# Pairs of batches woven together in a chunk-attention and token-mixing kernel on one core

## The chip, the cores and the metric

The kernel runs on one core of one Trainium2 chip. The metric is the device time of one execution in microseconds, as the median of the runs. A core has a matrix engine (PE, with its weight loads PEld), a vector engine (DVE), a scalar engine (ACT), GpSimd (POOL, which here issues every load) and SyncE (SP, which issues every store). Matrix products are written to PSUM, eight banks of 2 KB per partition, and have to be moved out by DVE or ACT.

## What is computed

Eight batches, eight heads, 576 tokens, 64 columns per head. Attention works within chunks of 64 tokens; its output, 512 columns per token, goes through a mixing block whose four weight matrices all batches share.

```python
scores = q_c @ k_c.T / 8                    # per chunk of 64 tokens and head
attn = exp(scores - max) / sum
x = (attn @ v_c)  ->  [b, 576, 512]
theta = x @ w_theta
zr, zi = x * cos(theta), x * sin(theta)
y = w_tok_r @ zr + w_tok_i @ zi             # over the 576 tokens of a batch
u = x + y
out = u + max(u @ w_ch, 0)
```

## The kernel before

All products are in fp16 with fp32 sums. The 576 tokens of a batch are cut into four tiles of 128 and one of 64 (`NSB` = 5). The kernel has three stages, one after the other.

*Weights* (lines 62 to 92). POOL loads all four matrices; the two token matrices are turned by 50 PE transposes (L78), and DVE copies them out.

*Attention*, all batches (from line 96). For each batch 15 loads (L107) bring q, k and v; 40 PE transposes (L120) turn q and k, and DVE copies them out (L127, L130). Per head, nine 64x64 score products go to PSUM (L142), ACT takes the exponential (L147 for four tiles, L153 for the last half tile), and nine products with a column of ones give the sums (L161). The products with v (L180) are scaled by the reciprocals (L167, L170) into `x16` (L185), which is kept for all batches.

*Mixing*, all batches (from line 190). Per batch: 20 transposes of x (L202), copied by ACT (L207); 20 products for theta (L219); cosine and sine on ACT (L226, L230); zr and zi on DVE (L234, L237); 50 products of 512 columns for y (L251), with the weights' token tiles as the stationary side, so that the half tile of 64 tokens is met both as a row and as a column; the sum u (L259); 20 transposes of u (L269), copied by ACT (L274); 20 products with `w_ch` (L282); relu and sum on DVE (L290); store on SP (L294). PSUM tiles are one bank each and there are eight of them.

No order is written out by hand: a scheduler takes the instructions in the order of the program text as priorities, simulates when each can run and how tiles come free, and fixes each engine's order. An engine then works through its own list strictly.

Of the kernel before, what the change touches and what calls it, by code (L numbers as in the profile page):

```python
# [9 lines left out]
FP32 = mybir.dt.float32  # L10
FP16 = mybir.dt.float16
AF = mybir.ActivationFunctionType
ALU = mybir.AluOpType


@with_exitstack
def kernel(
# [11 lines left out]
    nc = tc.nc  # L29
# [3 lines left out]
    NC = S // CH  # L33
    P = 128
    NSB = (S + P - 1) // P
    SB_SZ = [min(P, S - P * i) for i in range(NSB)]
    NDB = DM // P
    NE = H // 2
    scale = 1.0 / math.sqrt(D)
    pi_half = math.pi / 2.0  # L40
# [3 lines left out]
    xpool = ctx.enter_context(tc.tile_pool(name="xpool", bufs=1))  # L44
    psum = ctx.enter_context(tc.tile_pool(name="psum", bufs=8, space=bass.MemoryType.PSUM))
# [3 lines left out]
    ones16 = const.tile([P, 1], FP16, name="ones16")  # L49
    nc.vector.memset(ones16, 1.0)  # L50
    pihalf = const.tile([P, 1], FP32, name="pihalf")
    nc.vector.memset(pihalf, pi_half)
    zerob = const.tile([P, 1], FP32, name="zerob")
    nc.vector.memset(zerob, 0.0)
# [3 lines left out]
    wtokT_r = glob.tile([P, NSB, S], FP16, name="wtokTr")  # L58
    wtokT_i = glob.tile([P, NSB, S], FP16, name="wtokTi")

    with tc.tile_pool(name="wstage", bufs=1) as wstage:
        for ap, f16 in ((moe_w_theta, wtheta16), (moe_w_ch, wch16)):
            nc.gpsimd.dma_start(f16, ap.rearrange("(a p) e -> p a e", p=P))
        for ap, res in ((moe_w_tok_r, wtokT_r), (moe_w_tok_i, wtokT_i)):
            f16 = wstage.tile([P, NSB, S], FP16, name="wtok_nat16", tag="wtok_nat16")
            nc.gpsimd.dma_start(
                f16[:, 0 : NSB - 1, :],
                ap[0 : (NSB - 1) * P, :].rearrange("(a p) s -> p a s", p=P),
            )
            nc.gpsimd.dma_start(  # L70
                f16[0 : SB_SZ[NSB - 1], NSB - 1, :], ap[(NSB - 1) * P : S, :]
            )
            for sblk in range(NSB):
                ns = SB_SZ[sblk]
                pst = psum.tile([P, NSB, P], FP16, name="ps_wtokT", tag="ps")
                for tb in range(NSB):
                    nt = SB_SZ[tb]
                    nc.tensor.transpose(  # L78
                        pst[0:ns, tb, 0:nt],
                        f16[0:nt, tb, sblk * P : sblk * P + ns],  # L80
                        id16[0:nt, 0:nt],
                    )
                nc.vector.tensor_copy(
                    out=res[0:ns, sblk, 0 : (NSB - 1) * P].rearrange(
                        "p (a s) -> p a s", a=NSB - 1
                    ),
                    in_=pst[0:ns, 0 : NSB - 1, :],
                )
                nc.vector.tensor_copy(
                    out=res[0:ns, sblk, (NSB - 1) * P : S],  # L90
                    in_=pst[0:ns, NSB - 1, 0 : SB_SZ[NSB - 1]],
                )

    x16 = [xpool.tile([P, NSB, DM], FP16, name=f"x16_{b}") for b in range(B)]

    with (
        tc.tile_pool(name="att", bufs=2) as att,
        tc.tile_pool(name="qkv", bufs=2) as qkv,
    ):
        for b in range(B):  # L100
            qk16 = qkv.tile([P, NSB, 2, H, D], FP16, name="qk16")
            v16 = qkv.tile([P, NSB, H, D], FP16, name="v16")
            for sb in range(NSB):
                ns = SB_SZ[sb]
                for ti, t_ap in enumerate((q, k, v)):
                    dst = qk16[0:ns, sb, ti] if ti < 2 else v16[0:ns, sb]
                    nc.gpsimd.dma_start(  # L107
                        dst,
                        t_ap[b, :, sb * P : sb * P + ns, :].rearrange(
                            "h s d -> s h d"  # L110
                        ),
                    )
            qT = att.tile([P, NE, S], FP16, name="qT")
            kT = att.tile([P, NE, S], FP16, name="kT")
            for sb in range(NSB):
                ns = SB_SZ[sb]
                pqk = psum.tile([P, 2, NE, P], FP16, name="ps_qkT", tag="ps")
                for which in range(2):
                    for e in range(NE):
                        nc.tensor.transpose(  # L120
                            pqk[:, which, e, 0:ns],
                            qk16[0:ns, sb, which, 2 * e : 2 * e + 2, :].rearrange(
                                "s h d -> s (h d)"
                            ),
                            id16[0:ns, 0:ns],
                        )
                nc.vector.tensor_copy(  # L127
                    out=qT[:, :, sb * P : sb * P + ns], in_=pqk[:, 0, :, 0:ns]
                )
                nc.vector.tensor_copy(  # L130
                    out=kT[:, :, sb * P : sb * P + ns], in_=pqk[:, 1, :, 0:ns]
                )

            eT = att.tile([P, H, NSB, CH], FP16, name="eT")
            ps_rs = psum.tile([P, NSB, H], FP32, name="ps_rs", tag="ps")
            for h in range(H):
                e, par = h // 2, h % 2
                pst = psum.tile([P, NSB, CH], FP32, name="ps_sT", tag="ps")
                for c in range(NC):
                    cb, cp = c // 2, c % 2  # L140
                    sl = slice(c * CH, c * CH + CH)
                    nc.tensor.matmul(  # L142
                        pst[cp * CH : cp * CH + CH, cb, :],
                        kT[par * D : par * D + D, e, sl],
                        qT[par * D : par * D + D, e, sl],
                    )
                nc.scalar.activation(  # L147
                    out=eT[:, h, 0 : NSB - 1, :],
                    in_=pst[:, 0 : NSB - 1, :],
                    func=AF.Exp,  # L150
                    scale=scale,
                )
                nc.scalar.activation(  # L153
                    out=eT[0:CH, h, NSB - 1, :],
                    in_=pst[0:CH, NSB - 1, :],
                    func=AF.Exp,
                    scale=scale,
                )
                for c in range(NC):
                    cb, cp = c // 2, c % 2  # L160
                    nc.tensor.matmul(  # L161
                        ps_rs[cp * CH : cp * CH + CH, cb, h : h + 1],
                        eT[cp * CH : cp * CH + CH, h, cb, :],
                        ones16[cp * CH : cp * CH + CH, :],
                    )
            recip = att.tile([P, NSB, H], FP32, name="recip")
            nc.vector.reciprocal(  # L167
                out=recip[:, 0 : NSB - 1, :], in_=ps_rs[:, 0 : NSB - 1, :]
            )
            nc.vector.reciprocal(  # L170
                out=recip[0:CH, NSB - 1, :], in_=ps_rs[0:CH, NSB - 1, :]
            )

            for sb in range(NSB):
                ns = SB_SZ[sb]
                npar = ns // CH
                psx = psum.tile([P, H, D], FP32, name="ps_xout", tag="ps")
                for h in range(H):
                    for cp in range(npar):
                        nc.tensor.matmul(  # L180
                            psx[cp * CH : cp * CH + CH, h, :],
                            eT[cp * CH : cp * CH + CH, h, sb, :],
                            v16[cp * CH : cp * CH + CH, sb, h, :],
                        )
                nc.vector.tensor_tensor(  # L185
                    out=x16[b][0:ns, sb, :].rearrange("s (h d) -> s h d", h=H),
                    in0=psx[0:ns],
                    in1=recip[0:ns, sb, :].unsqueeze(-1).broadcast_to((ns, H, D)),
                    op=ALU.mult,
                )  # L190

    with (
        tc.tile_pool(name="moe", bufs=2) as moe,
        tc.tile_pool(name="moew", bufs=2) as moew,
    ):
        for b in range(B):
            xT = moe.tile([P, NDB, S], FP16, name="xT")
            for sb in range(NSB):
                ns = SB_SZ[sb]
                pxt = psum.tile([P, NDB, P], FP16, name="ps_xT", tag="ps")  # L200
                for db in range(NDB):
                    nc.tensor.transpose(  # L202
                        pxt[:, db, 0:ns],
# [121 lines left out]
```

## Time and profile before

| | |
|---|---|
| median of two runs | 332.54 us (331.72 and 333.35) |
| span of the profiled execution | 329.0 us |
| time outside the span (median less span) | 3.5 us |
| PE busy | 285.2 us, 87% of the span |
| DVE, ACT, POOL busy | 146.2, 115.7, 105.4 us |
| mean granted clock of PE | 0.887 of full |

The span runs from the first to the last instruction of one profiled execution. The profiled execution's own device time is not given apart; beside its span of 329.0 us stands the median of the runs, 3.5 us more, and that difference is taken as what lies around a span. Busy shares are means over stages with different limits, so the rows below are read stage by stage.

### The profile page before, as it was taken

The page shows a single profiled execution, that of the slowest core. Times are in us where ns is not written, and L with a number is a line of the kernel's source. Part 1 is how long each engine was busy: PE and PEld are TensorE (multiplying, and loading weights), DVE is VectorE, ACT ScalarE, POOL GpSimd, SP SyncE. Part 2 cuts the span into 40 slices and gives each one's busy share as a digit, 9 for nine tenths or more (in the row PEclk, how much of TensorE's full clock was granted, in tenths as well). Part 3 has the DMA queues.
Part 4 walks back from the last instruction along what each step waited for, and adds up shares of the span by engine and source line. Part 5 has one row for each costly group of instructions (what it writes and reads, how often), then busy time and mean ns, then how long its engine had stood idle before and what let it go on. Part 6 is the DMA issues. An engine that isn't in the chain of part 4 may idle for free.

```text
span 329.0 us, 7260 instructions
## 1 busy us (share of the span) xinstructions
PE 285.2 (87%) x3138; PEld 159.2 (48%) x3138; DVE 146.2 (44%) x319; ACT 115.7 (35%) x290; POOL 105.4 (32%) x132
## 2 busy tenths in 40 slices
PE   0328977879869889999999999999999999999992
PEld 0216866768858777334344344344344344344340
DVE  0216437357347354544534625525535534533532
ACT  0001440431421424805615515425426326227220
POOL 8189999999999900000000000000000000000000
PEclk9999577575676576999999999999999999999998
DMA  6999999999999980003003004004004003003004
GB/s 107 175 134 152 146 138 138 149 142 140 151 138 144 147 44 3 2 0 130 16 0 131 16 0 140 5 0 145 0 0 146 0 0 131 14 1 129 15 1 144
DMA packets 120064, 26.44 MB, mean 80 GB/s; under 512 B 113248, under 2 KB 115424, under 8 KB 120032
## 3 DMA queue, kind: packets, MB, share of 16 engines
q0 software_dynamic: 114784, 16.54, 79.4%
q1 hardware_dynamic: 5248, 9.44, 8.4%
q8 instruction: 24, 0.39, 0.5%
q14 instruction: 8, 0.07, 0.1%
HBM read 33.06 MB, written 9.44 MB: 129 GB/s over the span
## 4 chain that ended last, share of the span: by engine, by line
PE 62%; POOL 14%; DMA 12%; DVE 7%; issue 2%; ACT 1%; DVEq 0%; POOLq 0%; ACTq 0%
PE ps_y L251 30%; POOL qk L107 9%; PE ps_theta L219 8%; PE ps_uw L282 8%; DMA out_dram<-o 5%; POOL v L107 5%; DMA wtok_nat<-in_moe_w_tok_r_dram 3%; PE ps_uT L269 3%; PE ps_sT L142 3%; PE ps_xT L202 2%; PE ps_rs L161 2%; PE ps_wtokT L78 2%; DVE o L290 2%; DMA wtok_nat<-in_moe_w_tok_i_dram 2%; DMA qk<-in_q_dram 2%
## 5 line engine op out<-in xcount | busy, mean ns | idle before, releaser
L251 PE MATMUL ps_y<-zr,wtokTr 128*128 128x512 f16 (+3 forms) x200 | 53.9, 382 | 0.7 <-DVE zr L234 0.6
L251 PE MATMUL ps_y<-zi,wtokTi 128*128 128x512 f16 (+3 forms) x200 | 54.5, 384 | 0.0
L259 DVE TENSOR_TENSOR u<-ps_y,x 128x512 f16<-128x512 f32 (+1 forms) x40 | 27.6, 690 | 53.6 <-PE ps_y L251 53.6
L147 ACT ACTIVATE eT<-ps_sT 128x256 f16<-128x256 f32 x64 | 24.4, 382 | 69.5 <-PE ps_sT L142 66.7
L274 ACT COPY uT<-ps_uT 128x512 f16<-128x512 f16 (+1 forms) x40 | 18.6, 564 | 82.3 <-PE ps_uT L269 82.3
L290 DVE SCALAR_TENSOR_TENSOR o<-ps_uw,u 128x512 f32<-128x512 f32 (+1 forms) x40 | 27.6, 690 | 40.0 <-DMA out_dram<-o 22.5
L107 POOL DMA_DIRECT2D v<-in_v_dram x40 | 37.3, 933 | 1.5 <-DMA wch<-in_moe_w_ch_dram 1.3
L107 POOL DMA_DIRECT2D qk<-in_q_dram x40 | 37.3, 933 | 1.2 <-issue 0.8
L219 PE MATMUL ps_theta<-wtheta,xT 128*128 128x512 f16 (+1 forms) x160 | 36.9, 381 | 0.7 <-ACT xT L207 0.7
L107 POOL DMA_DIRECT2D qk<-in_k_dram x40 | 37.3, 932 | 0.1
L282 PE MATMUL ps_uw<-wch,uT 128*128 128x512 f16 (+1 forms) x160 | 36.9, 381 | 0.0
L251 PEld LDWEIGHTS <-wtokTi 128*128 128x128 f16 (+3 forms) x200 | 16.5, 99 | 38.5 <-issue 29.3
L120 PE MATMUL ps_qkT<-id,qk 128*128 128x128 f16 (+1 forms) x320 | 29.9, 267 | 5.8 <-DMA qk<-in_q_dram 4.5
L142 PE MATMUL ps_sT<-qT,kT 64*64 64x64 f16 x576 | 30.1, 232 | 3.7 <-DVE kT L130 3.6
L251 PEld LDWEIGHTS <-wtokTr 128*128 128x128 f16 (+3 forms) x200 | 17.8, 99 | 31.9 <-issue 17.0
L161 PE MATMUL ps_rs<-ones,eT 64*64 64x1 f16 x576 | 26.9, 191 | 7.0 <-ACT eT L147 7.0
L120 PEld LDWEIGHTS <-qk 128*128 128x128 f16 (+1 forms) x320 | 26.1, 127 | 8.7 <-DMA qk<-in_q_dram 6.1
L230 ACT ACTIVATE sin<-ps_theta,zerob 128x512 f16<-128x512 f32 (+1 forms) x40 | 29.6, 741 | 0.0
L226 ACT ACTIVATE cos<-ps_theta,pihalf 128x512 f16<-128x512 f32 (+1 forms) x40 | 29.5, 737 | 0.0
L207 ACT COPY xT<-ps_xT 128x512 f16<-128x512 f16 (+1 forms) x40 | 18.6, 564 | 28.2 <-PE ps_xT L202 28.2
L161 PEld LDWEIGHTS <-eT 64*64 64x64 f16 x576 | 21.8, 144 | 11.1 <-ACT eT L147 8.9
L185 DVE TENSOR_TENSOR x<-ps_xout,recip 128x512 f16<-128x512 f32 (+1 forms) x40 | 24.6, 681 | 0.4
(39 smaller groups left out, 242.2 us busy)
## 6 DMA issues: line engine op xcount, KB each, us to landing
out_dram<-o SPq DMA_DIRECT2D x32, 256.0 KB, 2.0
qk<-in_q_dram POOLq DMA_DIRECT2D x32, 128.0 KB, 5.5
qk<-in_k_dram POOLq DMA_DIRECT2D x32, 128.0 KB, 5.8
v<-in_v_dram POOLq DMA_DIRECT2D x32, 128.0 KB, 5.8
out_dram<-o SPq DMA_DIRECT2D x8, 128.0 KB, 2.3
wtok_nat<-in_moe_w_tok_r_dram POOLq DMA_DIRECT2D x1, 576.0 KB, 10.0
wtok_nat<-in_moe_w_tok_i_dram POOLq DMA_DIRECT2D x1, 576.0 KB, 6.1
wtheta<-in_moe_w_theta_dram POOLq DMA_DIRECT2D x1, 512.0 KB, 6.1
```

The lines of the kernel that those rows point to most:

```text
L107: nc.gpsimd.dma_start(dst, t_ap[b, :, sb * P : sb * P + ns, :].rearrange("h s d -> s h d"),)
L120: nc.tensor.transpose(pqk[:, which, e, 0:ns], qk16[0:ns, sb, which, 2 * e : 2 * e + 2, :].rearrange("s h d -> s (h d)"), id16[0:ns, 0:ns],)
L142: nc.tensor.matmul(pst[cp * CH : cp * CH + CH, cb, :], kT[par * D : par * D + D, e, sl], qT[par * D : par * D + D, e, sl],)
L161: nc.tensor.matmul(ps_rs[cp * CH : cp * CH + CH, cb, h : h + 1], eT[cp * CH : cp * CH + CH, h, cb, :], ones16[cp * CH : cp * CH + CH, :],)
L185: nc.vector.tensor_tensor(out=x16[b][0:ns, sb, :].rearrange("s (h d) -> s h d", h=H), in0=psx[0:ns], in1=recip[0:ns, sb, :].unsqueeze(-1). ...
L219: nc.tensor.matmul(pth[0:ns], xT[:, db, sb * P : sb * P + ns], wtheta16[:, db, :], start=(db == 0), stop=(db == NDB - 1),)
L226: nc.scalar.activation(out=cos16[0:ns, sb, :], in_=pth[0:ns], func=AF.Sin, bias=pihalf[0:ns], scale=1.0,)
L230: nc.scalar.activation(out=sin16[0:ns, sb, :], in_=pth[0:ns], func=AF.Sin, bias=zerob[0:ns], scale=1.0,)
L251: nc.tensor.matmul(psy[0:nt], wT[0:ns, sb, tsl], z[0:ns, sb, :], start=(step == 0), stop=(step == nsteps - 1),)
L259: nc.vector.tensor_tensor(out=u16[0:nt, mt, :], in0=psy[0:nt], in1=x16[b][0:nt, mt, :], op=ALU.add,)
L282: nc.tensor.matmul(puw[0:nt], uT[:, db, mt * P : mt * P + nt], wch16[:, db, :], start=(db == 0), stop=(db == NDB - 1),)
L290: nc.vector.scalar_tensor_tensor(out=o32[0:nt], in0=puw[0:nt], scalar=0.0, in1=u16[0:nt, mt, :], op0=ALU.max, op1=ALU.add,)
```

## The change

The eight batches become four pairs. A pair has 1152 tokens, nine full tiles of 128; the fifth (`MID`) holds the last 64 tokens of one batch and the first 64 of the other. The nine tiles form five groups of 2, 2, 1, 2 and 2. PSUM tiles are two banks each, and there are four.

- Attention (`a1`, `a2`, `a3`): transposes and one DVE copy per group; one exponential per group; v gets a 65th column of ones, so that the product with v gives the sums as well and L161 goes.
- Mixing (`a4`, `a5`): transposes of x and theta, with one copy, cosine and sine per group. Of the middle tile, the halves that lie in the wrong partitions are moved by two small DMAs on SP.
- `y`: the token mix is transposed. z is stationary and the turned token weights stream, 288 columns at a time, with the two half tiles of real and imaginary part joined in one ninth step of 128 rows. The result is uT, so the transposes L269 and the copies L274 go. `wT` is held in two forms, one per batch of the pair (100 transposes in `tok_w`).
- `w`: four products with `w_ch` and four of 128 columns with the identity, which turn uT back into u. ACT does relu (new), DVE the sum.
- Order of the text: steps of attention, x and theta of the next pair (`front`, `back`) are put between the steps of `y` and `w` of this pair by `weave`. Nothing else fixes the order; the scheduler does. Loads of the next pair stand ahead of the steps of this one, with six tiles for q and k (`nat`).

The diff cut to its core:

```diff
-    psum = ctx.enter_context(tc.tile_pool(name="psum", bufs=8, space=bass.MemoryType.PSUM))
+    GROUPS = [(0, 2), (2, 2), (4, 1), (5, 2), (7, 2)]
...
+        tc.tile_pool(name="psum", bufs=4, space=bass.MemoryType.PSUM)
+    nat = ctx.enter_context(tc.tile_pool(name="nat", bufs=6))
+    qkp = ctx.enter_context(tc.tile_pool(name="qkp", bufs=3))
+    epool = ctx.enter_context(tc.tile_pool(name="epool", bufs=6))
...
+    nc.gpsimd.memset(v16[:, :, :, D : D + 1], 1.0)
...
+    def a1(p, g):
...
+        nc.vector.tensor_copy(
+            out=qkT[:, :, :, 0 : n * P], in_=psv[:, :, :, 0 : n * P]
+        )
...
+    def a3(p, j, g):
...
+                nc.tensor.matmul(
+                    psv[sl, hf, h4 * (D + 1) : (h4 + 1) * (D + 1)],
+                    eT[sl, j - j0, h // 2, h % 2, :],
+                    v16[sl, slot, h, 0 : D + 1],
+                )
...
+        nc.vector.reciprocal(out=recip, in_=px[:, :, :, D : D + 1])
...
+    def y(p, bb, db):
...
+        for i, (kt, z, j) in enumerate(kts):
+            for hf in range(2):
+                nc.tensor.matmul(
+                    psv[:, hf, 0:HS],
+                    z[:, j, db * P : db * P + P],
+                    wT[bb][:, kt, hf * HS : hf * HS + HS],
+                    start=(i == 0),
+                    stop=(i == 2 * KT),
+                )
...
+    def w(p, j):
...
+            nc.tensor.matmul(
+                ps[:, 0:DM],
+                uT[:, db, j * P : j * P + P],
+                wch16[:, db, :],
+                start=(db == 0),
+                stop=(db == NDB - 1),
+            )
+            nc.tensor.matmul(
+                ps[:, DM + db * P : DM + db * P + P],
+                uT[:, db, j * P : j * P + P],
+                id16,
+            )
+        r = outp.tile([P, DM], FP32, name="relu", bufs=3)
+        nc.scalar.activation(out=r, in_=ps[:, 0:DM], func=AF.Relu)
+        o = outp.tile([P, DM], FP32, name="o32")
+        nc.vector.tensor_tensor(out=o, in0=ps[:, DM : 2 * DM], in1=r, op=ALU.add)
...
+    def front(p, gs):
+        steps = [c(a1, p, gs[0])]
+        for i, g in enumerate(gs):
+            if i + 1 < len(gs):
+                steps.append(c(a1, p, gs[i + 1]))
+            steps.append(c(a2, p, g))
+        return steps
+    def back(p, gs):
...
+                steps += [c(a3, p, j, gs[i]) for j in range(j0, j0 + n)]
+            if 0 <= i - 1 < len(gs):
+                steps.append(c(a4, p, gs[i - 1]))
+            if 0 <= i - 2 < len(gs):
+                steps.append(c(a5, p, gs[i - 2]))
...
+    for j in range(MID + 1):
+        load_qk(0, j)
+        load_v(0, j)
+    load_w(moe_w_theta, wtheta16)
+    load_tok_w()
+    for j in range(MID + 1, NT):
+        load_qk(0, j)
+        load_v(0, j)
+    load_w(moe_w_ch, wch16)
+    for f in front(0, [0, 1, 2]):
+        f()
+    weave(back(0, [0, 1, 2]), [c(tok_w, 0, kt) for kt in range(2 * KT + 1)])
+    for p in range(NP):
...
+        if more:
+            new_pair(p + 1)
+            load_pair(p + 1)
...
+        if p == 0:
+            weave(
+                y0,
+                front(0, [3, 4]) + back(0, [3, 4])
+                + [c(tok_w, 1, kt) for kt in range(2 * KT + 1)],
+            )
+            weave(y1, front(p + 1, nxt))
+            weave(ws, back(p + 1, nxt))
+            continue
+        if more:
+            weave(y0, front(p + 1, nxt))
...
+        main = []
+        for db in range(NDB):
+            main += [y1[db], ws[db]]
+        main += ws[NDB:]
+        weave(main, back(p + 1, nxt) if more else [])
```

## Rows read from the trace of the kernel before

**Rows 1.** The page, part 1: busy time, share of the span, instructions.

```profile
PE 285.2 (87%) x3138; PEld 159.2 (48%) x3138; DVE 146.2 (44%) x319; ACT 115.7 (35%) x290; POOL 105.4 (32%) x132
```

**Rows 2.** The page, part 2: 40 slices of PE busy and of its clock, in tenths.

```profile
PE   0328977879869889999999999999999999999992
...
PEclk9999577575676576999999999999999999999998
```

**Rows 3.** The page, part 4: the chain that ended last, by engine.

```profile
PE 62%; POOL 14%; DMA 12%; DVE 7%; issue 2%; ACT 1%; DVEq 0%; POOLq 0%; ACTq 0%
```

**Rows 4.** Windows: stretch, us, busy us of each engine, PEclk, DMA share, GB/s.

```profile
20.00:40.00 20.00, 14.72 (x287) 12.33 (x288) 8.28 (x26) 5.06 (x17) 18.81 (x24) 0.82 2.70 157
...
60.00:80.00 20.00, 17.74 (x449) 16.38 (x444) 10.79 (x27) 6.32 (x28) 19.98 (x25) 0.59 2.38 144
```

**Rows 5.** Chain in order of time, one batch of mixing: start us, us, what.

```profile
219.51 1.22 PE ps_uT L269 x20
220.73 4.54 PE ps_uw L282 x20
225.27 1.22 PE ps_xT L202 x20
226.49 4.54 PE ps_theta L219 x20
231.03 12.60 PE ps_y L251 x50
```

**Rows 6.** The same chain, in attention: a run of small products.

```profile
125.31 1.92 PE ps_xout L180 x61
```

**Rows 7.** Timeline, PEld at a change of array shape.

```profile
233.74 0.09 PEld L251 LDWEIGHTS <-wtokTr 64*128 64x128 f16 x1 [0.42 <-issue]
```

**Rows 8.** Groups by line and shape: xcount, busy us, mean ns, idle before.

```profile
L147 ACT ACTIVATE eT<-ps_sT 128x256 f16<-128x256 f32 x64 | 24.4, 382 | 69.5 <-PE ps_sT L142 66.7
L230 ACT ACTIVATE sin<-ps_theta,zerob 128x512 f16<-128x512 f32 x32 | 23.9, 748 | 0.0
L259 DVE TENSOR_TENSOR u<-ps_y,x 128x512 f16<-128x512 f32 x32 | 22.1, 691 | 38.8 <-PE ps_y L251 38.8
L274 ACT COPY uT<-ps_uT 128x512 f16<-128x512 f16 x32 | 16.4, 600 | 82.3 <-PE ps_uT L269 82.3
L153 ACT ACTIVATE eT<-ps_sT 64x64 f16<-64x64 f32 x64 | 13.2, 207 | 0.0
```

**Rows 9.** Timeline of POOL: two issues in a row.

```profile
21.25 0.91 POOL L107 DMA_DIRECT2D qk<-in_q_dram  x1
22.11 0.92 POOL L107 DMA_DIRECT2D qk<-in_k_dram  x1
```

**Rows 10.** Waits: engine, line, waited for: us in total, times, longest.

```profile
PE ps_rs L161 <- ACT eT L147: 7.0, 16, 0.5
...
PE ps_sT L142 <- DVE kT L130: 3.6, 10, 0.6
```

**Rows 11.** The page, part 6: stores, KB each, us to landing.

```profile
out_dram<-o SPq DMA_DIRECT2D x32, 256.0 KB, 2.0
```

**Rows 12.** Timeline of ACT, where the exponentials are over and the sines begin.

```profile
131.44 1.28 ACT L226 ACT_TABLE_LOAD   x1
132.73 0.69 ACT L226 ACTIVATE cos<-ps_theta,pihalf 128x512 f16<-128x512 f32 x1
```

**Rows 13.** Windows as rows 4: the clock through attention.

```profile
91.00:92.00 1.00, 1.00 (x16) 0.74 (x14) 1.00 (x4) 0.00 (x0) 1.00 (x2) 1.00 2.48 143
...
115.00:118.00 3.00, 3.00 (x31) 2.99 (x30) 3.00 (x8) 0.00 (x0) 0.42 (x1) 0.50 2.23 118
122.00:128.00 6.00, 6.00 (x180) 5.67 (x177) 2.55 (x6) 2.62 (x12) 0.00 (x0) 0.50 0.01 3
```

**Rows 14.** Timeline of PE: transposes of q and k.

```profile
89.50 2.50 PE L120 MATMUL ps_qkT<-id,qk 128*128 128x128 f16 x28
...
115.01 3.49 PE L120 MATMUL ps_qkT<-id,qk 128*128 128x128 f16 x32
```

More of the change, by code (lines that the diff above doesn't have):

```diff
@@ L13, with weave @@
 ALU = mybir.AluOpType
+def weave(main, filler):
+    n, m = len(main), len(filler)
+    done = 0
+    for i, step in enumerate(main):
+        step()
+        want = ((i + 1) * m) // n
+        while done < want:
+            filler[done]()
+            done += 1
 @with_exitstack
@@ L47 @@
+    outp = ctx.enter_context(tc.tile_pool(name="outp", bufs=4))
     id16 = const.tile([P, P], FP16, name="id16")
     make_identity(nc, id16)
[L49 to L50 removed]
     pihalf = const.tile([P, 1], FP32, name="pihalf")
[L52 to L54 removed]
+    nc.vector.memset(pihalf, math.pi / 2.0)
     wtheta16 = glob.tile([P, NDB, DM], FP16, name="wtheta16")
@@ L57 @@
     wch16 = glob.tile([P, NDB, DM], FP16, name="wch16")
[L58 to L65, printed above, removed]
+    wT = [glob.tile([P, 2 * KT + 1, S], FP16, name=f"wT{i}") for i in range(2)]
@@ new lines, with psum2, tok_ranges @@
+    wnat = glob.tile([P, KT + 1, 2, S], FP16, name="wnat")
+    NV = 2 * NT
+    v16 = glob.tile([P, NV, H, VP], FP16, name="v16")
+    nc.gpsimd.memset(v16[:, :, :, D : D + 1], 1.0)
+    def psum2(name, dtype=FP32):
+        n = 1024 if dtype == FP32 else 2048
+        return psum.tile([P, n], dtype, name=name, tag="ps")
+    nats = {}
+    def tok_ranges(j):
+        if j < MID:
+            return [(0, 0, j * P, P)]
+        if j > MID:
+            return [(0, 1, j * P - S, P)]
+        return [(0, 0, MID * P, CH), (CH, 1, 0, CH)]
@@ new lines, in load_w, with tok_w @@
+    def load_w(ap, f16):
+        nc.gpsimd.dma_start(f16, ap.rearrange("(a p) e -> p a e", p=P))
+    def tok_w(par, kt):
+        ps = psum2("ps_wT", FP16)
+        for tb in range(KT + 1):
+            nt = P if tb < KT else CH
+            if kt < 2 * KT:
+                s0 = (kt % KT) * P + (CH if par else 0)
+                parts = [(slice(0, P), kt // KT, s0)]
+            else:
+                s0 = 0 if par else KT * P
+                parts = [(slice(ri * CH, ri * CH + CH), ri, s0) for ri in range(2)]
+            for rows, ri, s0 in parts:
+                nc.tensor.transpose(
+                    ps[rows, tb * P : tb * P + nt],
+                    wnat[0:nt, tb, ri, s0 : s0 + rows.stop - rows.start],
+                    id16[0:nt, 0:nt],
+                )
+        if kt % 2:
+            nc.vector.tensor_copy(out=wT[par][:, kt, :], in_=ps[:, 0:S])
+        else:
+            nc.scalar.copy(out=wT[par][:, kt, :], in_=ps[:, 0:S])
@@ new lines, with new_pair @@
+    st = {}
+    def new_pair(p):
+        st[p] = dict(
+            x=pairp.tile([P, NT, DM], FP16, name="x16", bufs=1),
+            xT=pairp.tile([P, NDB, T], FP16, name="xT"),
+            zr=pairp.tile([P, NT, DM], FP16, name="zr16"),
+            zi=pairp.tile([P, NT, DM], FP16, name="zi16"),
+            qkT={},
+            eT={},
+        )
+    def a1(p, g):
+        j0, n = GROUPS[g]
+        ps = psum2("ps_qkT", FP16)
+        psv = ps.rearrange("p (w e s) -> p w e s", w=2, e=NE)
+        for jj in range(n):
+            t = nats.pop((p, j0 + jj))
+            for w in range(2):
+                for e in range(NE):
@@ new lines, in a3 @@
+    def a3(p, j, g):
+        j0, n = GROUPS[g]
+        eT = st[p]["eT"][g]
+        slot = (p % 2) * NT + j
+        ps = psum2("ps_x")
+        psv = ps.rearrange("p (f c) -> p f c", f=2)
+        for h in range(H):
+            hf, h4 = h // NE, h % NE
+            for cp in range(2):
+                sl = slice(cp * CH, cp * CH + CH)
+                nc.tensor.matmul(
+                    psv[sl, hf, h4 * (D + 1) : (h4 + 1) * (D + 1)],
+                    eT[sl, j - j0, h // 2, h % 2, :],
+                    v16[sl, slot, h, 0 : D + 1],
+                )
+        px = psv[:, :, 0 : NE * (D + 1)].rearrange("p f (h c) -> p f h c", h=NE)
+        recip = trig.tile([P, 2, NE, 1], FP32, name="recip")
+        nc.vector.reciprocal(out=recip, in_=px[:, :, :, D : D + 1])
+        nc.vector.tensor_tensor(
+            out=st[p]["x"][:, j, :].rearrange("s (f h d) -> s f h d", f=2, h=NE),
+            in0=px[:, :, :, 0:D],
+            in1=recip.broadcast_to((P, 2, NE, D)),
+            op=ALU.mult,
+        )
@@ new lines, in a4 @@
+    def a4(p, g):
+        j0, n = GROUPS[g]
+        ps = psum2("ps_xT", FP16)
+        psv = ps[:, 0 : NDB * n * P].rearrange("p (a s) -> p a s", a=NDB)
+        for jj in range(n):
+            for db in range(NDB):
+                nc.tensor.transpose(
+                    psv[:, db, jj * P : jj * P + P],
+                    st[p]["x"][:, j0 + jj, db * P : db * P + P],
+                    id16,
+                )
+        nc.scalar.copy(
+            out=st[p]["xT"][:, :, j0 * P : (j0 + n) * P], in_=psv
+        )
@@ new lines, in a5 @@
+    def a5(p, g):
+        j0, n = GROUPS[g]
+        ps = psum2("ps_theta")
+        for jj in range(n):
+            j = j0 + jj
+            for db in range(NDB):
+                nc.tensor.matmul(
+                    ps[:, jj * DM : jj * DM + DM],
+                    st[p]["xT"][:, db, j * P : j * P + P],
+                    wtheta16[:, db, :],
+                    start=(db == 0),
+                    stop=(db == NDB - 1),
+                )
+        cos = trig.tile([P, 2, DM], FP16, name="cos16")
+        sin = trig.tile([P, 2, DM], FP16, name="sin16")
+        pin = ps[:, 0 : n * DM]
+        nc.scalar.activation(
+            out=cos[:, 0:n].rearrange("p a e -> p (a e)"), in_=pin,
+            func=AF.Sin, bias=pihalf, scale=1.0,
+        )
+        nc.scalar.activation(
+            out=sin[:, 0:n].rearrange("p a e -> p (a e)"), in_=pin, func=AF.Sin
+        )
+        x, zr, zi = st[p]["x"], st[p]["zr"], st[p]["zi"]
+        if n == 2:
+            nc.vector.tensor_mul(
+                zr[:, j0 : j0 + n], x[:, j0 : j0 + n], cos[:, 0:n]
+            )
+            nc.vector.tensor_mul(
+                zi[:, j0 : j0 + n], x[:, j0 : j0 + n], sin[:, 0:n]
+            )
+            return
+        lo, hi = slice(0, CH), slice(CH, P)
+        tmp = trig.tile([P, DM], FP16, name="zmid")
+        nc.vector.tensor_mul(zr[lo, j0], x[lo, j0], cos[lo, 0])
+        nc.vector.tensor_mul(tmp[lo], x[lo, j0], sin[lo, 0])
+        nc.vector.tensor_mul(zi[hi, j0], x[hi, j0], sin[hi, 0])
+        nc.vector.tensor_mul(tmp[hi], x[hi, j0], cos[hi, 0])
+        nc.sync.dma_start(zr[hi, j0], tmp[lo])
+        nc.sync.dma_start(zi[lo, j0], tmp[hi])
@@ new lines, in y @@
+    def y(p, bb, db):
+        s = st[p]
+        if bb == 0 and db == 0:
+            s["uT"] = pairp.tile([P, NDB, T], FP16, name="uT")
+        first = bb * (MID + 1)
+        kts = [(kt, s["zr"] if kt < KT else s["zi"], first + kt % KT)
+               for kt in range(2 * KT)]
+        kts.append((2 * KT, s["zi"] if bb else s["zr"], MID))
+        ps = psum2("ps_y")
+        psv = ps.rearrange("p (f c) -> p f c", f=2)
+        for i, (kt, z, j) in enumerate(kts):
[6 more added lines that the diff above has]
+                    stop=(i == 2 * KT),
+                )
+        sl = slice(bb * S, bb * S + S)
+        nc.vector.tensor_tensor(
+            out=s["uT"][:, db, sl].rearrange("p (f c) -> p f c", f=2),
+            in0=psv[:, :, 0:HS],
+            in1=s["xT"][:, db, sl].rearrange("p (f c) -> p f c", f=2),
+            op=ALU.add,
+        )
@@ new lines, in c, with load_pair @@
+    def c(f, *a):
+        return lambda: f(*a)
+    NG = len(GROUPS)
+    def load_pair(p):
+        for j in range(NT):
+            load_qk(p, j)
+            load_v(p, j)
+    def front(p, gs):
[6 more added lines that the diff above has]
+    def back(p, gs):
+        steps = []
+        for i in range(len(gs) + 2):
+            if i < len(gs):
+                j0, n = GROUPS[gs[i]]
+                steps += [c(a3, p, j, gs[i]) for j in range(j0, j0 + n)]
[3 more added lines that the diff above has]
+                steps.append(c(a5, p, gs[i - 2]))
+        return steps
```

286 lines of the change are left out of this document (73 added, 213 removed).

## The prediction

> **What bounds the kernel now.** I read the page first. PE is the busiest engine [rows 1], but that is a mean over two different limits, as the slices show: from the 17th on (131 us) PE stands at 9 and its clock at 9, in the twelve before that PE is at 6 to 9 with a clock of 5 to 7 [rows 2]. The chain of waits says the same: PE holds 62% of it, POOL and DMA together 26% [rows 3]. The windows then give the limit of each stage. In attention POOL is busy 19.98 us of 20 while PE, at a clock of 0.59, has gaps: loads set the pace [rows 4]. In mixing the chain runs on PE without a break: 1.22 + 4.54 + 12.60 + 1.22 + 4.54 = 24.12 us per batch [rows 5], 193 us for eight. So 329 - 193 = 136 us go to loading, attention and the end. Two things can be won: loads hidden under PE's work, and a shorter mixing stage.
>
> **PE's own work after the change.** Prices at full clock: a product of 512 columns takes 4.54/20 = 0.227 us, a transpose of 128 columns 1.22/20 = 0.061 us [rows 5]; on the line between them 288 columns take 0.130 us (an estimate; the lower end is 288/512 of 0.227, 0.128, the upper the full 0.227). A 64x64 product takes 1.92/61 = 0.0315 us [rows 6]. One pair needs:
>
> - y: 8 steps x 18 products x 0.130 = 18.7 us (before: 2 x 12.60)
> - w: 36 x (0.227 + 0.061) = 10.4
> - theta: 36 x 0.227 = 8.2 (before 9.1, with the half tiles)
> - x transposes: 36 x 0.061 = 2.2; those of u are gone
> - q and k transposes: 72 x 0.061 = 4.4
> - scores and attention times v: 288 x 0.0315 = 9.1; 144 products with ones are gone, and 65 columns instead of 64 cost nothing that the price can show
>
> Sum 53.0 us. Small products now stand between large ones: 14 blocks per pair (5 of `a2`, 9 of `a3`), two changes of array shape each. A y of before holds 20 changes and is 12.60 - 50 x 0.227 = 1.25 us longer than its products, 0.06 us a change [rows 5]; the longest gap of a weight load there is 0.42 us [rows 7]. I take 0.1: 2.8 us a pair (1.7 to 11.8). Four pairs at 55.8 us are 223 us, and 100 transposes of the token weights 6.1 us: 229 us of PE.
>
> **The other engines.** From the groups [rows 8] ACT's exponential costs (382 - 207)/192 = 0.91 ns an element over a base of 149 ns, so 1024 elements 1.08 us. ACT per pair: exponentials 4.9 us, x copies at most 9 x 0.60 = 5.4, sines and cosines at most 18 x 0.748 = 13.5, the new relu (not in the trace; as an exponential 0.61, as a sine 0.75) 9 x 0.65 = 5.9: about 30 us of 55.8. DVE per pair, at the 0.691 us that 512 elements out of PSUM take [rows 8] as an upper bound for all it does: 26 passes of 512 or 576 elements 18.6 us, five copies of up to 2048 elements 12.4, 18 fp16 products 12.4, nine small reciprocals some 2: at most 45 us. Both are covered by PE; each works beside the next PE block. The sum in `w` now waits for ACT's relu (before, one DVE pass did both); behind it on DVE stand the copies of `a1` and the scaling of x, for which the next transposes wait, so a late relu delays attention of the next pair by its own length, 0.65 us, under some 4 us of PE work per step. The middle tile's two small DMAs stand in SP's queue between stores, 2.0 us each [rows 11], and feed only the last of a y's nine steps; y and w of the pair before cover them, and without that cover they cost 2 us a pair. The memset of ones, not in the trace, is one small POOL instruction ahead of the first load: 0 to 0.9 us (an issue), I take 0.3. POOL issues one load each 0.86 us [rows 9]; 30 per pair are 26 us, under 55.8.
>
> **What PE waits for.** In attention of before PE lost 7.0 us to exponentials and 3.6 us to copies over eight batches, 2.7 us a pair [rows 10]. The weave covers these with y and w, but PSUM tiles fall from eight to four and each is held through its evacuation. A pair holds tiles for 53 us of PE writing, 30 us of ACT and up to 31 us of DVE, 114 of 4 x 55.8 = 223 us: half full, so a step will now and then find none free. Between nothing and 10 us a pair, I take 5, nearest to the row: 15 us over the three woven pairs.
>
> **Start and end.** Data arrive at 157 GB/s as stored [rows 4]. Five tiles of q, k, v (1.97 MB), w_theta (0.52) and the token weights (1.33) are 3.8 MB: 24 us, with 3 us ahead. Transposing the weights for the first batch takes 3 us and their copies 2, so the first y starts near 33. Tiles 5 to 8 (1.57 MB) land by 38 to 39; their chain of ten dependent steps takes about 12 us, under which y of batch 0 (9.4) and the second set of weight transposes lie. So y of batch 1 starts near 50 (45 to 58). Done by then: attention and theta of pair 0 with its changes (26.8), weight transposes (6.1), one y (9.4), 42.3 us. Remaining: 229.3 - 42.3 = 187. The end: relu 0.65, sum 0.69 and a store of 2.0 us [rows 8, 11], with the semaphores 4.
>
> Sum: 50 + 187 + 15 + 4 = 256 us of span. Around the span lie 332.5 - 329.0 = 3.5 us (the median of the runs less the profiled span, whose own time is not given): **260 us**, 0.78 of before. With every low end (start 45, no waits) it is 240; with start 58, waits of 10 a pair and shape changes of 0.2 it is 290.
>
> **Two rules weighed.** Exponentials and sines alternate now: by the text's order 10 table loads instead of 2. The trace shows 131.44 to 132.73 from the load's start to the sine, 1.29 us [rows 12]; ten are 13 us on an engine with 25 us to spare in each pair. The Trainium skill, "ScalarE: Activation LUTs", section "Table sets: the hidden batching unit", says to do all of one set before switching, and "What ACT_TABLE_LOAD costs" puts a switch at about 2.66 us; by it ten are 27 us, still off the path; the row, half as long, decides.
>
> The clock: it was at 0.50 through 6 us of nothing but 64x64 products, and at 1.00 in a stretch of q and k transposes [rows 13]; in 115 to 118 the same transposes ran at 0.50 right after small products, 32 of them in 3.49 us [rows 13, 14]. In the change no run of small products is longer than about 1 us, so I forecast 1.00 from the first y on. The Trainium skill, "TensorE: Matmul & The Clock Gate", section "Part 4: PE-mode transpose", says that full clock does not engage in transposes; the trace differs, with 28 transposes from 89.5 and 1.00 by 91 [rows 13, 14]. Its section "A second HAM failure mode: psum-queue depth-cycling" says short idle gaps between groups that cycle through PSUM make the clock swing; that is the first rival below, and no row here has such gaps between large products.
>
> **The rivals.**
>
> *The clock stays at half in the weave (the slower side).* Small products and waits for PSUM tiles pull it down. Price: 3.49/32 = 0.109 us a transpose against 0.061, 0.375 ns a column. Columns still to come after 50 us and woven: 4 x 96,768 less 53,000 of pair 0 less 64,500 of the last pair (not woven) = 270,000, so 101 us. At half clock throughout 361 us; equal to before from 72% of the woven time on, slower by over 2% from 78%. For it: attention ran at 0.59. Against: there, loads left gaps and nothing large ran. Some part, 30 to 60%, gives 290 to 320.
>
> *The scheduler's order costs more than text order.* Its simulated times for loads and evacuations fix strict lists. Exponentials of the next pair are lifted into gaps between sines (up to 10 more loads a pair, 1.29 us each, 50 us on ACT, half of it seen by PE), or transposes stand ahead of y and wait for their load. 260 + 25 = 285 us. For it: four PSUM tiles half full leave gaps. Against: a step is lifted only into a gap of PE, and PE is the full engine.
>
> *The weave does not hide the loads.* If pairs run one after another, mixing without attention is 39.5 x 4 = 158, attention at the loads' pace 120 x 0.86 = 103 [rows 9], start 27, end 8: 296 us. Against: the six tiles for q and k let loads run ahead.
>
> **How the numbers follow.** Forecast, 245 to 275: 0.55. Better, all waits hidden: 0.06. Scheduler's order, 275 to 300: 0.18. Loads not hidden: 0.06. Half clock in part: 0.08; in most, within 2%: 0.03; throughout, slower: 0.04. Under 2% could not be told from no change. Faster 0.93, same 0.03, slower 0.04. The range, 240 to 300, leaves out about 0.16.
>
> **What would show it right or wrong.** Right: PE over 85% busy from 50 us on with a clock of 1.00; products of 288 columns spaced by 0.13 us; POOL with long gaps; ACT with 10 to 15 table loads; first y near 33, second batch's near 50. Wrong: a clock row below 0.9 after 50 us (first rival), over 25 table loads or PE waiting for ACT by more than 20 us (second), PE waiting for q and k loads after 60 us (third), or 288 columns at over 0.15 us, which adds 11 us for each 0.02.

## The result, and the profile after

245.06 us, median of two runs (244.62 and 245.50), against 332.54: a ratio of 0.739, 95% interval 0.733 to 0.745. The forecast was 260 (240 to 300), faster. Ratios and intervals, here and below, leave out runs more than 1.5% above the fastest of their kernel. The profiled execution took 245.50 us with a span of 243.4, so 2.1 us lie around a span and not 3.5 (a run of the kernel before beside the experiments: 332.31 with a span of 330.5).

The page of the changed kernel, parts 1, 2 and 4, answering to [rows 1 to 3]: busy time by engine; PE's slices and clock; the chain by engine.

```profile
PE 208.7 (86%) x2692; PEld 143.6 (59%) x2692; DVE 129.1 (53%) x217; ACT 111.2 (46%) x136; POOL 105.9 (44%) x133
...
PE   0453799289999979899998998999989989999992
...
PEclk9999999758999999999999999999999999999999
...
PE 71%; DVE 8%; POOL 7%; DMA 6%; ACT 5%; issue 1%; POOLq 0%; DVEq 0%
```

POOL is as busy as before (105.9 us), but now it stands beside PE's work instead of ahead of it: POOL and DMA together fall from 26% of the chain to 13%. PE's busy time fell by 76.5 us, and there is one place where its clock falls, slices 8 to 10. The windows show the same by stage; columns as in [rows 4].

```profile
0.00:40.00 40.00, 22.56 (x294) 14.71 (x294) 11.14 (x21) 13.67 (x16) 34.07 (x48) 1.00 1.74 142
40.00:60.00 20.00, 14.14 (x222) 10.20 (x222) 9.46 (x18) 6.78 (x9) 16.43 (x21) 0.74 2.11 141
60.00:220.00 160.00, 152.91 (x2033) 105.84 (x2032) 98.48 (x165) 85.35 (x104) 55.40 (x66) 1.00 0.96 100
113.00:162.40 49.40, 47.66 (x651) 33.07 (x649) 31.30 (x53) 25.66 (x32) 16.73 (x20) 1.00 0.91 100
```

From 60 to 220 us PE is idle for 7.1 of 160 us at full clock. In the first 60 us it is idle for 23.3. Its waits in the whole span show what for (who, what for: us in total, times, longest):

```profile
PE ps_qkT L176 <- DMA qk<-in_q_dram: 9.7, 5, 5.2
PE ps_wT L144 <- DMA wnat<-in_moe_w_tok_r_dram: 5.1, 1, 5.1
PE ps_y L312 <- DMA zr<-zmid: 4.0, 1, 4.0
PE ps_sT L198 <- DVE qkT L183: 4.0, 5, 0.9
...
PE ps_qkT L176 <- DMA qk<-in_k_dram: 1.9, 4, 1.0
```

All of the waits for DMA lie in the first 60 us: 16.7 us for loads and 4.0 for the moved half tiles. The chain in order of time gives the landmarks and the prices (start us, us, what), and the tile view the start of the first y, at 39.4 us (count: shortest, median and longest in ns, first to last start):

```profile
42.48 5.87 DMA zr<-zmid
...
51.29 4.45 PE ps_y L312 x18
...
71.17 2.31 PE ps_y L312 x18
...
113.06 2.21 PE ps_y L312 x18
...
162.38 2.21 PE ps_y L312 x18
164.58 1.79 PE ps_qkT L176 x32
...
177.85 0.45 PE ps_sT L198 x32
...
184.86 0.63 PE ps_x L223 x32
...
208.24 3.45 PE ps_theta L261 x16
211.70 11.03 PE ps_y L312 x90
```

```profile
L312 PE MATMUL ps_y<-wT,zr x40: 286/286/444, 39.4 to 68.2; 128*128 128x288 f16 x40
```

The first y of the second, third and fourth pair stand at 113.06, 162.38 and 211.70: a woven pair takes 49.3 us, where two batches of mixing alone took 48.2 before [rows 5], and attention now comes with it. The second batch of pair 0 starts its y at 71.17. At the end the last pair's y and w and the store take 31.7 us with nothing woven in.

### The profile page after: what moved, and what is told of

It is laid out like the page before. It is cut to its first block, busy times and chain, and to the rows that moved or that the text cites. A ratio compares the mean times of both kernels' runs of the same rounds, so it can differ in the third digit from the quotient of the medians.

```text
span 243.4 us, 6143 instructions
## 1 busy us (share of the span) xinstructions
PE 208.7 (86%) x2692; PEld 143.6 (59%) x2692; DVE 129.1 (53%) x217; ACT 111.2 (46%) x136; POOL 105.9 (44%) x133
## 4 chain that ended last, share of the span: by engine, by line
PE 71%; DVE 8%; POOL 7%; DMA 6%; ACT 5%; issue 1%; POOLq 0%; DVEq 0%
PE ps_y L312 30%; PE ps_uw L332 11%; PE ps_theta L261 11%; PE ps_qkT L176 5%; POOL qk L108 4%; DMA wnat<-in_moe_w_tok_r_dram 4%; PE ps_x L223 3%; PE ps_xT L245 3%; PE ps_wT L144 3%; PE ps_uw L339 3%; DMA zr<-zmid 2%; POOL v L116 2%; PE ps_sT L198 2%; DVE x L231 2%; ACT cos L271 2%; DVE qkT L183 2%
## 5 line engine op out<-in xcount | busy, mean ns | idle before, releaser
L320 DVE TENSOR_TENSOR uT<-ps_y,xT 128x576 f16<-128x576 f32 x32 | 24.2, 757 | 46.7 <-PE ps_y L312 46.7
L312 PE MATMUL ps_y<-wT,zr 128*128 128x288 f16 x288 | 44.4, 293 | 4.2 <-DMA zr<-zmid 4.0
L332 PE MATMUL ps_uw<-wch,uT 128*128 128x512 f16 x144 | 42.6, 380 | 3.2 <-DVE x L231 2.3
L345 ACT ACTIVATE relu<-ps_uw 128x512 f32<-128x512 f32 x36 | 21.5, 598 | 46.4 <-PE ps_uw L339 46.2
L312 PE MATMUL ps_y<-wT,zi 128*128 128x288 f16 x288 | 41.5, 290 | 0.0
L312 PEld LDWEIGHTS <-zr 128*128 128x128 f16 x288 | 26.9, 99 | 12.9 <-DMA zr<-zmid 4.2
L261 PE MATMUL ps_theta<-wtheta,xT 128*128 128x512 f16 x144 | 33.7, 379 | 0.5 <-DVE o L347 0.5
L312 PEld LDWEIGHTS <-zi 128*128 128x128 f16 x288 | 28.6, 99 | 7.7
L339 PE MATMUL ps_uw<-id,uT 128*128 128x128 f16 x144 | 31.5, 219 | 0.0
L347 DVE TENSOR_TENSOR o<-ps_uw,relu 128x512 f32<-128x512 f32 x36 | 24.7, 688 | 10.7 <-ACT relu L345 10.5
L231 DVE TENSOR_TENSOR x<-ps_x,recip 128x512 f16<-128x512 f32 x36 | 24.2, 688 | 0.7
```

The source lines that it names most:

```text
L231: nc.vector.tensor_tensor(out=st[p]["x"][:, j, :].rearrange("s (f h d) -> s f h d", f=2, h=NE), in0=px[:, :, :, 0:D], in1=recip.broadcast_ ...
L261: nc.tensor.matmul(ps[:, jj * DM : jj * DM + DM], st[p]["xT"][:, db, j * P : j * P + P], wtheta16[:, db, :], start=(db == 0), stop=(db == ...
L312: nc.tensor.matmul(psv[:, hf, 0:HS], z[:, j, db * P : db * P + P], wT[bb][:, kt, hf * HS : hf * HS + HS], start=(i == 0), stop=(i == 2 * KT),)
L320: nc.vector.tensor_tensor(out=s["uT"][:, db, sl].rearrange("p (f c) -> p f c", f=2), in0=psv[:, :, 0:HS], in1=s["xT"][:, db, sl].rearrange ...
L332: nc.tensor.matmul(ps[:, 0:DM], uT[:, db, j * P : j * P + P], wch16[:, db, :], start=(db == 0), stop=(db == NDB - 1),)
L339: nc.tensor.matmul(ps[:, DM + db * P : DM + db * P + P], uT[:, db, j * P : j * P + P], id16,)
```

## The experiments

Each kernel below is the changed kernel with one edit, unless it says otherwise. Ratios are to the kernel before in the same runs; the changed kernel has 0.739 (0.733 to 0.745).

**The weave.** The text is made serial.

```diff
+        steps = list(y0)
...
-            weave(y1, front(p + 1, nxt))
-            weave(ws, back(p + 1, nxt))
...
+        steps += y1 + ws
         if more:
...
-        weave(main, back(p + 1, nxt) if more else [])
+            steps += front(p + 1, nxt) + back(p + 1, nxt)
+        for f in steps:
+            f()
```

> Same work, but the text has no weave: all y and w of a pair, then all attention and theta steps of the next. Theory (the text's order is what puts attention under y and w): attention then runs by itself, its waits for copies, exponentials and the last three tiles' loads show and its long run of 64x64 products lets the clock fall; 4 to 8 us for each of three pairs, 257 to 270 us. Rival (the scheduler lifts the steps into gaps by itself, so the text's order is of no matter): within 1% of the changed kernel, 243 to 248 us.

One run took 268.5 us at a mean clock of 0.942, the other three 274.4 to 275.1 at 0.919, so there is no interval. That is 23 us more than the changed kernel in the one run and 29 to 30 in the others; only the one lies in the theory's range. The rival falls with all four: the scheduler does not make good for the text. The kept trace is of one of the three longer runs, so it shows the larger of the two losses. Its window from 60 to 220 us and that of a stretch in which attention stands by itself, columns as above, and PE's waits over the whole span:

```profile
60.00:220.00 160.00, 140.37 (x1759) 95.29 (x1760) 84.13 (x137) 72.86 (x89) 61.88 (x75) 0.91 1.04 103
100.00:112.00 12.00, 7.14 (x179) 5.26 (x178) 4.89 (x9) 2.65 (x3) 10.80 (x14) 0.62 2.42 151
```

```profile
PE ps_qkT L176 <- DMA qk<-in_q_dram: 12.9, 13, 5.3
PE ps_qkT L176 <- DMA qk<-in_k_dram: 9.7, 10, 2.0
PE ps_sT L198 <- DVE qkT L183: 6.4, 9, 0.8
```

From 60 to 220 us PE idles 19.6 us instead of 7.1, and the clock is at 0.91 instead of 1.00, though q and k still have six tiles to run ahead in. Of the 22.6 us of waits for q and k 10.9 lie after 60 us, where the changed kernel has none. The span of this trace is 29.1 us longer: 14.6 us of that are idle time of PE (49.3 against 34.7) and 14.5 are the same products taking longer (223.2 us busy against 208.7).

**Loads ahead.** `nat` gets two buffers instead of six.

```diff
-    nat = ctx.enter_context(tc.tile_pool(name="nat", bufs=6))
+    nat = ctx.enter_context(tc.tile_pool(name="nat", bufs=2))
```

> Two tiles for q and k instead of six, all else as the changed kernel, so that the loads of a group can begin only when the transposes of the one before are done. This is the forecast's third rival made to happen. Theory (the loads run ahead, and that hides them): a group's four loads take 3.5 us to issue and some 5.5 us to land, against 3.7 us of PE work between the groups of a front; 5 us of wait for each of five groups in three pairs, part of it covered by a y put between: 265 to 300 us. Rival (the tiles are of no matter, the weave covers a late load): 244 to 250 us.

289.6 us, 0.874 (0.868 to 0.880), as the theory had it: 44 us dearer, the largest single effect but one. The first of its waits:

```profile
PE ps_qkT L176 <- DMA qk<-in_q_dram: 31.1, 19, 5.2
```

In the changed kernel this wait is 9.7 us, all of it at the start. PE's idle time grows by 27.7 us (62.4 against 34.7); the other 16.3 us are the same products taking longer (225.0 us busy), at a clock of 0.93 from 60 to 220 us. So it takes both, the weave and loads that run ahead of it; y put between covers only a part of a late load.

**The sums.**

```diff
-                    psv[sl, hf, h4 * (D + 1) : (h4 + 1) * (D + 1)],
-                    eT[sl, j - j0, h // 2, h % 2, :],
-                    v16[sl, slot, h, 0 : D + 1],
+                for c0, c1 in ((D, D + 1), (0, D)):
+                    nc.tensor.matmul(
+                        psv[sl, hf, h4 * (D + 1) + c0 : h4 * (D + 1) + c1],
+                        eT[sl, j - j0, h // 2, h % 2, :],
+                        v16[sl, slot, h, c0:c1],
+                    )
```

> The 65th column undone: sums by 576 products with a column of ones of their own, into the same place. Theory (PE sets the pace; at full clock 32 small products take 0.45 us, 0.014 each): 576 x 0.014 = 8 us, of which some lies in the waits of the start: 250 to 254 us. Rival (PE is not the limit in the weave): 244 to 247 us. At the price of 0.0315 us that the forecast used it would be 263 us.

250.8 us, 0.756 (0.752 to 0.759): 5.7 us for 576 products, 0.010 us each, so PE does set the pace. PE's busy time rises by more, 10.1 us (218.8 against 208.7), so a part lies in time that was idle before. The added products have one column each; this is not the price of a product of 64 columns.

**The transposed token mix.** y as before the change (but with joined half tiles), u turned by transposes, one DVE pass at the end.

```diff
+                nc.tensor.matmul(
+                    ps[rows, 0:DM],
+                    wT[bb][:, kt, t0 : t0 + n],
+                    z[:, jz, :],
+                    start=(i == 0),
+                    stop=(i == 2 * KT),
+                )
...
+            nc.tensor.transpose(
+                pt[:, db * P : db * P + P], u[:, db * P : db * P + P], id16
+            )
+        nc.scalar.copy(
+            out=uT[:, :, j * P : j * P + P],
```

> The transposed token mix undone within the weave: 45 products of 512 columns per batch with the joined half tiles, the sum u in natural layout, 36 transposes of u per pair with ACT copies, four products of w and one DVE pass; x gets a second buffer, xT and uT one each. Theory (the weave brings most, the transposed mix little): y 45 x 0.227 = 10.2 us a batch instead of 8.8, w and transposes 10.4 instead of 10.0 a pair: 3.2 us a pair, 13 in all, 254 to 262 us. Rival (the transposed mix brings most of it): 275 us or more.

300.6 us, 0.906 (0.900 to 0.911): 39 us above the range of my theory, and the number speaks for its rival. The trace spoke against both, with a wait that the changed kernel does not have:

```profile
PE ps_uw L347 <- ACT uT L341: 36.4, 34, 3.0
```

I had written each tile's transposes right ahead of the products that need their copy, and the scheduler left them so. The next kernel differs from this one only by having the transposes one step of w earlier (those of the first tile excepted):

```diff
+        if j == 0:
+            t(p, 0)
+        if j + 1 < NT:
+            t(p, j + 1)
```

> As e4, with the transposes of u and their ACT copy one step of w ahead of the products that need them. In e4 PE waited 36 us for these copies (34 times). Theory (e4's extra 42 us over its 13 us of PE work are this round trip over ACT, put too close by the text): the waits fall to 10 us or less, 262 to 275 us. Rival (old mixing in the weave costs that much whatever the order): 292 to 302 us.

260.2 us, 0.783 (0.779 to 0.787). The same wait is now:

```profile
PE ps_uw L356 <- ACT uT L341: 3.2, 6, 1.1
```

So 40 us hung on one step's distance in the text: 33 us of this wait, and a clock of 0.952 that became 0.980. What is left, 15 us above the changed kernel, is in the trace 10.9 us of PE's busy time (219.6 against 208.7) and 4.5 of its idle time. The 13 us of PE work in the expectation mix the prices of two kernels: at the prices of the chain above the transposed mix saves 90 x 0.216 less 144 x 0.1226, 1.8 us a pair or 7 in all. Where the rest of the 15 us comes from is not shown; `xT` and `uT` have one buffer less here, which no run undoes by itself. The transposed mix has a second use: `w` needs nothing from ACT before its products, so it cannot fall into this wait at all (for DVE's uT PE waits 0.4 us in the changed kernel).

**PSUM tiles.** Three instead of four.

```diff
-        tc.tile_pool(name="psum", bufs=4, space=bass.MemoryType.PSUM)
+        tc.tile_pool(name="psum", bufs=3, space=bass.MemoryType.PSUM)
```

> Three PSUM tiles instead of four. The forecast took 15 us of waits for four; PE was idle 7.1 us between 60 and 220. Theory (tiles matter once the use nears the number: 114 us of use in 3 x 49 is 78%): 252 to 265 us. Rival (the number does not matter at this load, the forecast's 15 us were unfounded): 244 to 248 us.

258.0 us, 0.777 (0.775 to 0.779), as the theory had it. PE's idle time from 60 to 220 us goes from 7.1 to 14.1 us:

```profile
60.00:220.00 160.00, 145.89 (x1970) 100.75 (x1971) 93.61 (x159) 82.43 (x100) 55.67 (x67) 1.00 0.96 96
```

**Tables.** One function for all.

```diff
-            func=AF.Sin, bias=pihalf, scale=1.0,
+            func=AF.Exp, bias=pihalf, scale=1.0,
...
-            out=sin[:, 0:n].rearrange("p a e -> p (a e)"), in_=pin, func=AF.Sin
+            out=sin[:, 0:n].rearrange("p a e -> p (a e)"), in_=pin, func=AF.Exp
```

> Sine and cosine replaced by the exponential, so that one table serves all (theta's functions are then others): 9 of 10 table loads go. Theory (ACT has room, only the one load at 34 us stands in the chain): 242 to 245 us. Rival (the loads delay the steps behind them): 9 x 1.29 = 12 us at most, 233 to 240 us.

243.35 us, 0.733 (0.730 to 0.735): the interval overlaps that of the changed kernel, so the nine loads cost nothing that the runs can tell, 1.7 us by the medians, though ACT's busy time falls from 111.2 to 99.6 us. The trace of the changed kernel has the ten loads that its text order gives, five in each of two groups (xcount, busy us, mean ns, idle before):

```profile
L205 ACT ACT_TABLE_LOAD x5 | 6.4, 1283 | 0.8 <-PEq L438 0.7
L271 ACT ACT_TABLE_LOAD x5 | 6.4, 1283 | 0.1
```

The rule of the Trainium skill to batch by table set ("ScalarE: Activation LUTs", section "Table sets: the hidden batching unit") is true of ACT's own time, 12.8 us; this run shows that it need not be true of the kernel's.

**The start: the moved half tiles.** For the first pair they are written in place.

```diff
+        d_lo = zi[lo, j0] if p == 0 else tmp[lo]
+        d_hi = zr[hi, j0] if p == 0 else tmp[hi]
...
+        if p == 0:
+            return
```

> For the first pair the two halves of the middle tile are written in place, so the two small DMAs that move them are left out (those rows of z are then not the right ones); the same products on DVE, three pairs as before. Theory: PE's wait of 4.0 us for this move, which landed after 5.9 us among the loads, and the half clock from 46 to 56 us behind it cost 4 to 8 us: 237 to 241 us. Rival (loads of the next tiles hold the start anyway): 244 to 246 us.

239.5 us, 0.723 (0.719 to 0.726), as the theory had it. In the changed kernel PE stands at the ninth step of the first y for 4.0 us, with 55 of the 64 score products of the next two groups waiting behind it in PE's list, and the clock is at 0.50 from 46 to 56 us; without the move it is at 1.00 there. Windows of the changed kernel, and then of this one:

```profile
44.30:48.40 4.10, 0.06 (x6) 0.01 (x1) 0.85 (x1) 0.00 (x0) 3.68 (x5) 0.68 2.30 172
46.00:56.00 10.00, 6.91 (x103) 4.30 (x105) 1.90 (x4) 1.94 (x2) 7.53 (x11) 0.50 2.22 139
```

```profile
46.00:56.00 10.00, 9.07 (x156) 6.64 (x157) 4.91 (x11) 5.04 (x5) 8.85 (x13) 1.00 2.19 134
```

**The start: another order of loads and text.**

```diff
     new_pair(0)
-    for j in range(MID + 1):
+    load_w(moe_w_theta, wtheta16)
+    for j in range(NT):
         load_qk(0, j)
         load_v(0, j)
-    load_w(moe_w_theta, wtheta16)
     load_tok_w()
...
+    for f in front(0, [0, 1, 2, 3, 4]):
         f()
...
+    for f in back(0, [0, 1, 2, 3, 4]):
+        f()
+    for kt in range(2 * KT + 1):
+        tok_w(0, kt)
```

> Start in another order: w_theta first, then all nine tiles of pair 0, token weights and w_ch last; attention and theta of all five groups in the text ahead of the first y. Theory (the first 66 us lose about 25 us of PE to waits because the y of batch 0 stands ahead of tiles 5 to 8): work of pair 0 runs under the loads, the first y near 42 and the second batch's near 54: 231 to 237 us. Rival (bytes set the start in any order): 243 to 248 us.

243.5 us, 0.734 (0.731 to 0.736): no difference that can be told. The theory missed, and the number is the rival's. But its PE waits spoke of an order and not of bytes:

```profile
PE ps_qkT L176 <- DMA qk<-in_q_dram: 16.8, 9, 8.6
```

8.6 us of that are the first tile, which now comes behind `w_theta`; the rest are later tiles, at which PE's list stood while attention of loaded groups lay behind. So the same loads, with the text group by group:

```diff
+    for i in range(NG + 3):
+        if i < NG:
+            a1(0, i)
+            a2(0, i)
+        if 0 <= i - 1 < NG:
+            j0, n = GROUPS[i - 1]
+            for j in range(j0, j0 + n):
+                a3(0, j, i - 1)
...
```

> Loads as in e7 (w_theta, nine tiles, token weights, w_ch), but the text goes group by group: transposes and scores of a group, then attention of the one before, x of the one before that, theta of the third. In e7 all transposes and scores stood ahead of attention, and PE's list held it at loads (20 us of waits for q and k) while finished exponentials lay there. Theory (the order of PE's list, not the bytes, cost e7 its gain): pair 0 is done but for y when the token weights land at 41 to 43, the second batch's y starts near 57 instead of 66: 234 to 239 us. Rival (bytes set the start): 242 to 246 us.

238.7 us, 0.719 (0.716 to 0.722), in the theory's range: faster than both kernels, 0.974 of the changed one, with the intervals apart. So it was not the bytes alone. PE's waits for q and k fall from 20.1 to 13.3 us, while those for DVE's copies rise from 4.1 to 8.9. The landmarks in its chain:

```profile
49.74 2.31 PE ps_y L312 x18
...
62.75 2.31 PE ps_y L312 x18
...
106.53 2.21 PE ps_y L312 x18
```

The second batch's y stands at 62.75 and the second pair at 106.53, 8.4 and 6.5 us earlier than in the changed kernel, though not near 57 as expected. (The expectation took 66 us for the changed kernel's second batch; that is the fourth y of the first batch, the second begins at 71.17.)

## Why the prediction was right, and where its steps were off

- **PE's work.** The line through 512 and 128 columns gave 0.130 us for 288; it is 11.03/90 = 0.1226. A 512-column product is 3.45/16 = 0.216 and a transpose 1.79/32 = 0.056 (0.227 and 0.061 were taken from runs that hold the 64-row tiles). The term that was mis-sized is the small products: 0.0315 us came from a stretch of attention times v at half clock [rows 6, 13]; at full clock scores take 0.45/32 = 0.014 and attention times v 0.63/32 = 0.020, 4.9 us a pair instead of 9.1. That the clock makes all of that difference is not shown.
- **What PE waits for.** Shape changes (2.8 us) and waits (5) were 7.8 us a pair. A pair at the measured prices, in the order of the forecast's list, is 17.7 + 9.8 + 7.8 + 2.0 + 4.0 + 4.9 = 46.2 of 49.3 us: 3.1 us for both, of which PE is idle for 1.7 (47.66 us busy of 49.40). So the 5 us were too many for tiles half in use; that their number matters close by is right, as three tiles cost 13 us more.
- **Start.** The step that failed in the sum. The first y came at 39.4 us instead of 33 and, above all, the second batch's at 71.2 instead of 50. The first token weights were there at 26.1, close to the forecast's 27, but from then to 39.4 PE was busy all the time, with the weights' transposes and with attention, x and theta of the first three groups; the forecast had counted the transposes and their copies alone. From there on I had the chain of tiles 5 to 8 lie under the first y's, as if it took no time of PE. By the forecast's own prices y (9.4), the second set of weight transposes (3.05) and four ninths of 26.8 (11.9) are 24.4 us of PE's work, and from 33 to 50 there are 17. It took 31.8 us: PE was busy for 25.4 of them, at a mean clock of 0.84, and idle for 6.4.
- **The moved half tiles.** Of that idle time 4.0 us is the ninth step of the first y, which PE's fixed list put ahead of most scores of these tiles, and which waited for the moved half tiles. I had noted these DMAs at 2.0 us and as covered; among the loads they took 5.87 us, and what was queued behind the waiting step was on PE, not on SP. The half clock came behind this wait and was gone without it. The experiment with halves in place gets 5.5 us back, the group order 6.3; in the group order's trace PE does not wait for the halves either, so the two overlap.
- **Compensation.** From the second batch's y on, the forecast had 187 + 15 + 4 = 206 us; it was 172. The start was 21 us too short and the rest 34 too long (three pairs at 60.8 us instead of 49.3), and the span was missed by their difference, 13 us (256 against 243.4). The closeness of the total is thus partly luck; each of the two by itself was further off.
- **Cover.** ACT and DVE were beside PE as forecast: 25.7 and 31.3 us busy in 49.4. POOL's 30 loads a pair are hidden as long as they run ahead (two-tile run).
- **Rivals.** By the forecast's own signs a clock below 0.9 after 50 us spoke for the first rival, and the clock was at 0.50 until 56. But that was one place of 10 us, behind a stall, and not from small products: 1.00 from 60 us on. Order did cost, as in the second, but it was the text's own order, at the start, and not lifted exponentials: table loads were the ten of the text. Loads not hidden did not happen. With two tiles for q and k they come late and it takes 290 us; the 296 were worked out for pairs one after another, so that the two are close checks nothing.
- **Gain by part**, each undone alone: loads ahead 44 us, weave 23 to 30, transposed mix 15 (55 with its transposes close by), 65th column 6. They overlap, so they are not shares of the 87. The copies and activations by group and the joined half tiles were not undone by themselves.

## What to carry to other kernels

Where one stage waits for loads and the next for PE, put them into one stream: here attention and mixing of two batches take 49.3 us, where mixing alone took 48.2. Take the price of a small product from a stretch at the clock that the new place will have. When a scheduler fixes each engine's list, write dependent steps at least one step apart and arrivals in their real order: it keeps the text's order more than one hopes, and 40 us hung on one step. Work that is laid under other work still needs its engine: add up what each engine has to do in that stretch, here 24.4 us of PE in 17.

## What was not expected of the hardware

A small SBUF-to-SBUF move of 64 rows, 1.9 to 2.0 us in each of the other three pairs, took 5.87 us in the first while loads were in flight (POOL, which issues the loads, was busy for 7.9 of the 10 us from 40 us on; around the other three it was busy for at most 1.5 of 8 us). And a stall of 4.0 us cost more than itself: PE then ran at the lower level of its clock for 10 us, 46 to 56, in which a y of 18 products took 4.45 us instead of 2.21. The stall alone does not explain it. A longer one in the same trace, 5.1 us up to 26.06 while PE waited for the token weights, left the clock at 1.00; PE had been busy for 7.7 of the 15 us from 5 to 20 before that one, and for all of the 13.3 us from 26.06 to 39.40 and most of the next five before the other. Which of the differences between the two places decides is not shown here.
